# A fused attention and MLP block on one core: a half of chunk 1's second norm transposed by DMA, and two weight loads gated later

## The chip, the cores and the metric

The kernel runs on one NeuronCore of a Trainium2 chip. The metric is the device time of one execution in microseconds, the median of several runs. The profile shows one execution by itself.

## What is computed

One transformer block in bfloat16, for x of 1 x 2048 x 512. Attention is local and dilated: 32 heads of 16 features, and each position attends to itself and to the seven positions 2, 4, ..., 14 before it. The MLP is a gated one with F = 1376 hidden features.

```python
def _A_ref(x, wqkv, wo):            # S = 2048, D = 512, H = 32, Dh = 16
    W, dil = 8, 2
    q, k, v = ...(x @ wqkv) split in heads
    idx = pos[:, None] - (arange(W) * dil)[None, :]     # masked where < 0
    logits = einsum("bhsd,bhswd->bhsw", q, k[idx]) * Dh ** -0.5
    o = einsum("bhsw,bhswd->bhsd", softmax(logits), v[idx])
    return o.reshape(B, S, D) @ wo

def _B_ref(x, W_gate, W_up, W_down):
    gate = x @ W_gate
    return ((gate * (gate > 0)) * (x @ W_up)) @ W_down

h = x + _A_ref(_layernorm(x), wqkv, wo)
out = h + _B_ref(_layernorm(h), W_gate, W_up, W_down)
```

## The kernel before, in words

**Tiles and stages.** The 2048 rows are cut in four chunks of 512 rows, each of four blocks of 128 rows. All weights stay in on-chip memory once they are loaded. Each chunk goes through the same stages:

- *First norm* (the function `layernorm`, line 433). Mean and variance come from L467 on VectorE, the scale from two small ScalarE steps (L477, L480). The normalized row is written either by ScalarE (L499) or by VectorE (L502).
- *Transposing.* The matrix products want the features on the partitions, so each normalized block of 128 x 512 is transposed into a `quad` tile of 128 x 4 x 512. That happens in one of two ways. On TensorE it takes four transposes per block (L531, two blocks to a PSUM bank) and an eviction of the bank by ScalarE (L547). By DMA it takes one transposing transfer per block on SP's queue (L520). The table `DMAT` (L378) lists the pairs of blocks that go by DMA: ('h',1,0) stands for the second norm ("h") of chunk 1, blocks 0 and 1. All pairs that it doesn't list go by TensorE.
- *Query, key and value products* (L572, four matmuls of 512 columns each). ScalarE evicts them (L580): queries into a `quad` tile, keys into `kT`, values into `vT`. `kT` and `vT` are one tile each for all four chunks.
- *Scores.* VectorE multiplies queries with the keys of four window offsets at once (L620; four products to a chunk, each over two of the four feature groups of `kT` and written to a `big` tile; chunk 0 has smaller ones, L635). TensorE sums over the features (L626, 16 matmuls for half of the window), and ScalarE takes the exponential (L684).
- *Denominator and weights.* In chunks 1 to 3 VectorE adds the two halves (L716) and TensorE sums them with one matmul (L701). ScalarE forms the reciprocal (L707, L710). In these chunks VectorE scales the weights (L728), and eight broadcasting DMAs on SP (L744) spread them over the features into a `big` tile; in chunk 0 the sums are scaled at the end (L783).
- *Weighted sum.* VectorE multiplies with the values (L776, L791 in chunk 0). A tree of three additions follows: in chunks 0 to 2 the first one is an accumulating DMA on POOL's queue (L819), the others are VectorE's (L779, and L813 for the last one in chunks 1 to 3).
- *Output product and residual.* Four output products (L855) take four matmuls each. In chunk 0 a fifth matmul per block adds x by the identity (L858) and ScalarE evicts the bank with a row sum (L864); in the others VectorE adds x (L866).
- *Second norm*: the row sum gives the mean (L448, VectorE), ScalarE squares (L456), then scale, normalized rows (L502, VectorE) and transposes as above.
- *MLP.* Up and gate products (L928, 20 of four matmuls in a chunk), evicted by ScalarE (L932 and, with the ReLU, L935), multiplied by VectorE (L956). The last 96 features of F go through a tail of their own (L895 to L914, with one DMA transpose). The down product (L978, 11 matmuls to a block) is evicted by ScalarE and added to x by a DMA on POOL in chunks 0 and 1 (L987, L1012), and added by VectorE in chunks 2 and 3 (L991).

**Loads of weights.** W_up and W_down ("ud" in `LATE`) aren't loaded in the set-up. A small gate operation `lg` on POOL (L836) copies a few elements from the tile of chunk 0's last sum into both weight tiles. The loads overwrite these elements and so must wait for the gate. Two transfers for W_up and then the ones for W_down are issued on SP after it (`f_load`).

**What sets the order.** The body of the kernel only collects operations. `Plan.order` (L115) then simulates the engines (TensorE, VectorE, ScalarE, POOL, SP) with the durations and the DMA model that the file states, and emits the operations in the order of their simulated starts. The table `RANK` (L18) gives every operation a rank by the number in which it was collected; each engine takes its operations strictly by rank. So the order on one engine is that of `RANK`, and the simulation only decides how the engines' lists are interleaved when they are emitted. The framework then draws the semaphore waits from the order of emission: what is emitted later and touches the same tile waits for what was emitted earlier.

All chunks are interleaved: while chunk 0 is in its MLP, chunk 1 is in its attention, and so on. TensorE's list around the change, with the times of the profile before: query, key and value products of chunks 0 to 2 up to 49, among them the scores of chunk 0 and 1; the four output products of chunk 0 from 49.5 to 55, each between other products; the value products of chunk 2; chunk 0's up and gate products from 65; its down products among chunk 1's output products (85 to 91); chunk 1's second norm, its eight transposes at 96.2, and its up and gate products behind them.

Of the kernel before, what the change touches and what calls it, by code (L numbers as in the profile page):

```python
# [16 lines left out]

RANK = [  # L18
# [38 lines left out]
]  # L57


# [33 lines left out]
class Plan:  # L93
# [9 lines left out]
    def add(self, key, *a, **k):  # L103
        op = Op(*a, **k)
        op.key = key
        op.seq = len(self.ops)
        if RANK:
            op.prio = RANK[op.seq]
        self.ops.append(op)
        for b in set(op.take) | set(op.use):  # L110
            b.left += 1
        return op


    def order(self):  # L115
        waiting = list(self.ops)
        free = {}
# [7 lines left out]
        while left:  # L125
# [27 lines left out]
            for eng, cands in best.items():  # L153
                first = min(t for t, _ in cands)
                t, op = min(
                    ((t, op) for t, op in cands if t <= first + self.LOOK.get(eng, 0.02)),
                    key=lambda x: (x[1].prio, x[1].seq),
                )
                if pick is None or t < pick[0]:
                    pick = (t, op)  # L160
            t, op = pick
            op.start, op.done = t, t + op.dur + op.lat
            held = 0.0
            if op.dq:
                at, sw, busy = t + op.dur + op.dq[0], free.get("DQ", 0.0), op.dq[1]
                if op.eng == "POOL":
                    late = 1.0 if at < free.get("DT", -1.0) + 0.3 else 0.0
                    at = free["DQ"] = max(at, sw) + late + busy
                else:
                    turn = 0.6 < busy < 0.9  # L170
                    at = max(at, free.get("DQ" + op.eng, 0.0))
                    if at < sw + (0.3 if turn else 0.0):
                        share = 0.03 if turn else 0.18
                        late = max(sw - at, 0.0)
                        at += busy / share if late * share >= busy else late + busy - late * share
                        free["DQ"] = sw + (1.65 if turn else 0.5 * busy)
                        held = at + op.lat - 4.5
                    else:
                        at += busy
                    free["DQ" + op.eng] = at  # L180
                    if turn:
                        free["DT"] = at
                op.done = at + op.lat
            free[op.eng] = max(t + op.dur, held)
# [18 lines left out]
def kernel(  # L203
# [11 lines left out]
    nc = tc.nc  # L215
# [4 lines left out]
    NT = D // P  # L220
# [9 lines left out]
    LATE = "ud"  # L230
# [5 lines left out]
    NFT = NFF + (1 if FTAIL else 0)  # L236
# [32 lines left out]
    wgu_sb = sb.tile([P, NT, 2, F], BF16, name="wgu_sb")  # L269
    wd_sb = sb.tile([P, NFT, D], BF16, name="wd_sb")  # L270
# [93 lines left out]
    add = plan.add  # L364
# [10 lines left out]
    NHALF = 6  # L375
    XT = (3.5, 3.65, 5.6, 6.1, 8.5, 8.9, 9.4, 9.9, 15.9, 17.4)
    WT = (7.55, 7.55, 5.0, 14.2, 18.7, 25.5, 22.0, 29.0)
    DMAT = (('h',2,0),('h',2,2),('h',3,0),('h',3,2),('h',1,0),('x',3,0),('x',3,2))  # L378

    EARLY = (1, 2, 3)  # L380

# [31 lines left out]
    wload = {n: [load(t)] for n, t in zip(("q", "k", "ab", "v", "o", "u", "g", "d"), WT)}  # L413
# [141 lines left out]
    for tk in range(NCK):  # L555
# [10 lines left out]
        for n, (c, t) in enumerate(seq):  # L566
# [16 lines left out]
            if tk == 0 and n < NHALF:  # L583

                a = None
                for i, (lo, hi, d0, d1, evs) in enumerate(((0, 2 * P, 0, 2, xev[0:2]), (0, 2 * P, 2, NT, []), (2 * P, CS, 0, NT, xev[2:]))):
                    a = add(("qk%s%d" % ("abc"[i], n), tk), "PE", MM * (d1 - d0) * (hi - lo) / CS + 0.005,
                            lambda f=f_mm, lo=lo, hi=hi, d0=d0, d1=d1: f(lo, hi, d0, d1),
                            evs + [wload["ab"][0] if i == 0 else wl, a, fills[-1]], pr - 5,
                            take=[mm], use=[xnT], lat=PEL if i == 2 else 0.0)  # L590
            else:
                a = add(("qkv%d" % n, tk), "PE", 4 * MM, f_mm, xev + [wl], pr, take=[mm], use=[xnT], lat=PEL)
# [9 lines left out]
        apr = base + 20  # L602
# [130 lines left out]
        ab, abd = Buf(ab_s), []  # L733
# [99 lines left out]
            if tk not in EARLY:  # L833
                oev[t] = add(("om%d" % t, tk), "DVE", D2, f_om, [m, rcd], tpr, take=[OT], use=[mt, rc], lat=DL)
        if tk == 0 and LATE:
            def f_lg(mt=mt):  # L836
                nc.gpsimd.tensor_copy(out=wgu_sb[0:1, :, 1, 0:1], in_=mt.t[0:1, 0:1, 0:NT].rearrange("p a s -> p s a"))
                nc.gpsimd.tensor_copy(out=wd_sb[0:1, :, 0:1], in_=mt.t[0:1, 0:1, 0:NFT].rearrange("p a s -> p s a"))

            lg = add(("lg", tk), "POOL", 0.3, f_lg, [oev[NT - 1]], apr, use=[mt], lat=0.1)  # L840
            for n in LATE:
                for i in range(2):
                    wload[n].append(add(("ld" + n, i), "SP", 0.45 + 0.1 * (n == "d" and i), lambda n=n, i=i: f_load(n, i),
                                        [lg], 0, lat=0.5, dq=(1.0, 1.74)))
        for t in range(NT):
            kdone["v", tk, t] = vd[t]

# [217 lines left out]
```

## Time and profile before

| | |
|---|---|
| time, median of 3 runs | 197.32 us (197.26 to 197.83) |
| the profiled execution, its own time | 195.9 us |
| span of the profiled execution | 193.9 us |
| TensorE busy | 189.1 us (98%) |
| VectorE busy | 147.4 us (76%) |
| ScalarE busy | 119.0 us (61%) |
| POOL busy | 16.9 us (9%) |

The span reaches from the first to the last instruction of the profiled execution; its own time is longer by what lies around that. The median belongs to other executions. In the lines of the profile, PE is TensorE, DVE is VectorE, ACT is ScalarE and SP issues DMAs; L and a number is a line of the kernel. A line of a timeline has the start and the length in microseconds (a group of like instructions in one line), the engine, the line, the operation, the tiles out<-in, and in brackets a wait ahead of it and what released it. In a line of the chain of waits the two numbers are the start and the length of one step.

### The profile page before, as it was taken

To read this page: it belongs to the slowest core of one execution; us is meant where nothing else is said; L and a number is where in the kernel's file an instruction comes from. 1 tells how busy PE (TensorE), PEld (TensorE's weight loads), DVE (VectorE), ACT (ScalarE), POOL (GpSimd) and SP (SyncE) were. 2 spreads that over 40 slices of the span, in tenths; PEclk is the share of its full clock that TensorE was granted. 3 is DMA by queue.
4 is the path that set the end of the run, shared out by engine and by line. 5 is a ranking of instruction groups with operands and counts; after the bars stand their busy time and mean duration, and the time that the engine had idled before them with its cause. 6 is when DMAs were issued, how large, how long until landed. Compare 5 with 4: busy or idle time off the path is not lost.

```text
span 193.9 us, 3084 instructions
## 1 busy us (share of the span) xinstructions
PE 189.1 (98%) x1133; PEld 98.7 (51%) x1133; DVE 147.4 (76%) x237; ACT 119.0 (61%) x245; POOL 16.9 (9%) x35
## 2 busy tenths in 40 slices
PE   7999999999999999999999999999999999999994
PEld 7886454554345445444444454444444645544543
DVE  6999999979999999988998658899965321404432
ACT  3689999973997777665346858505658803445600
POOL 3000002510000023100033110003000000000000
PEclk9999999999999999999999999999999999999999
DMA  6889475999508657926366998222400460004103
GB/s 200 240 261 392 133 182 96 196 194 261 217 0 192 163 108 149 176 50 156 79 126 132 193 183 175 54 54 40 71 0 0 99 198 3 0 0 136 53 3 108
DMA packets 25214, 24.61 MB, mean 127 GB/s; under 512 B 11408, under 2 KB 21488, under 8 KB 25200
## 3 DMA queue, kind: packets, MB, share of 16 engines
q1 hardware_dynamic: 22176, 16.26, 30.5%
q0 software_dynamic: 2304, 7.34, 20.9%
q10 hardware_dynamic: 720, 0.82, 1.2%
q8 instruction: 9, 0.15, 0.3%
q14 instruction: 5, 0.04, 0.1%
HBM read 8.42 MB, written 2.10 MB: 54 GB/s over the span
## 4 chain that ended last, share of the span: by engine, by line
PE 88%; DVE 4%; ACT 3%; DMA 1%; issue 1%; DVEq 0%
PE bank L928 36%; PE bank L978 20%; PE bank L572 14%; PE bank L855 7%; PE bank L626 4%; PE bank L895 3%; PE bank L421 3%; DVE big L620 2%; PE bank L531 2%; ACT row L499 2%; DMA quad<-row 1%; DVE big L779 1%; ACT kT L580 1%; DVE quad L783 1%; PE bank L858 0%
## 5 line engine op out<-in xcount | busy, mean ns | idle before, releaser
L928 PE MATMUL bank<-quad,wgu_sb 128*128 128x512 bf16 x320 | 71.7, 379 | 0.0
L928 PEld LDWEIGHTS <-wgu_sb 128*128 128x128 bf16 x320 | 31.1, 98 | 37.1 <-issue 0.8
L978 PE MATMUL bank<-wd_sb,gT 128*128 128x512 bf16 (+3 forms) x198 | 39.7, 355 | 0.0
L935 ACT ACTIVATE gr<-bank 128x512 bf16<-128x512 f32 x40 | 23.7, 604 | 15.5 <-PE bank L928 13.0
L932 ACT CAST up_sb<-bank 128x512 bf16<-128x512 f32 x40 | 23.0, 590 | 15.8 <-PE bank L928 13.9
L572 PE MATMUL bank<-quad,wqk_sb 128*128 128x512 bf16 (+1 forms) x152 | 29.6, 345 | 0.8 <-DMA quad<-row 0.4
L978 PEld LDWEIGHTS <-gT 128*128 128x128 bf16 (+1 forms) x198 | 18.4, 98 | 19.8 <-issue 0.4
L620 DVE TENSOR_TENSOR big<-quad,kT 128x4096 bf16<-128x4096 bf16 x12 | 27.3, 2285 | 1.0 <-ACT kT L580 0.9
L776 DVE TENSOR_TENSOR big<-big,vT 128x4096 bf16<-128x4096 bf16 x12 | 27.2, 2283 | 0.0
L572 PEld LDWEIGHTS <-wqk_sb 128*128 128x128 bf16 x152 | 16.7, 113 | 11.3 <-issue 1.1
L956 DVE TENSOR_TENSOR gT<-gr,up_sb 128x1024 bf16<-128x1024 bf16 x20 | 13.7, 688 | 9.4 <-ACT gr L935 7.4
L991 DVE TENSOR_TENSOR row<-x_sm,bank 128x512 bf16<-128x512 bf16 (+2 forms) x10 | 5.5, 579 | 19.0 <-PE bank L978 19.0
L819 POOL DMA_DIRECT2D big<-big x12 | 10.5, 931 | 84.0 <-DVE big L776 55.9
L779 DVE TENSOR_TENSOR big<-big 128x1024 bf16<-128x1024 bf16 (+2 forms) x24 | 17.2, 730 | 0.6 <-DMA big<-big 0.3
L572 PE MATMUL bank<-quad,wv_sb 128*128 128x512 bf16 x64 | 15.7, 380 | 0.0
L855 PE MATMUL bank<-wo_sb,quad 128*128 128x512 bf16 x64 | 15.0, 379 | 0.1
L547 ACT COPY quad<-bank 128x1024 bf16<-128x1024 bf16 (+1 forms) x10 | 8.6, 888 | 5.6 <-PE bank L531 5.6
L456 ACT ACTIVATE row<-x_sm,mv 128x512 bf16<-128x512 bf16 x12 | 8.6, 716 | 4.3 <-DVE mv L448 4.2
L866 DVE SCALAR_TENSOR_TENSOR x_sm<-x_sm,bank 128x512 bf16<-128x512 bf16 x12 | 8.1, 684 | 3.9 <-PE bank L855 3.9
L467 DVE BATCH_NORM_STATS2 st<-x_sm 128x6 f32<-128x512 bf16 x16 | 10.4, 676 | 0.6 <-DMA x_sm<-in_A_x_dram 0.5
L580 ACT CAST kT<-bank 128x512 bf16<-128x512 f32 x16 | 9.2, 598 | 2.6 <-DVE big L620 1.9
L580 ACT CAST quad<-bank 128x512 bf16<-128x512 f32 x16 | 8.9, 599 | 2.5 <-PE bank L572 2.5
(77 smaller groups left out, 169.9 us busy)
## 6 DMA issues: line engine op xcount, KB each, us to landing
big<-big POOLq DMA_DIRECT2D x12, 512.0 KB, 4.9
big<-ex SPq DMA_DIRECT2D x32, 128.0 KB, 2.9
wgu_sb<-in_B_W_gate_dram SPq DMA_DIRECT2D x2, 688.0 KB, 9.3
wgu_sb<-in_B_W_up_dram SPq DMA_DIRECT2D x2, 688.0 KB, 8.3
wd_sb<-in_B_W_down_dram SPq DMA_DIRECT2D x2, 640.0 KB, 6.3
x_sm<-in_A_x_dram SPq DMA_DIRECT2D x2, 512.0 KB, 6.3
x_sm<-up_sb POOLq DMA_DIRECT2D x4, 256.0 KB, 4.4
out_dram<-x_sm SPq DMA_DIRECT2D x4, 256.0 KB, 2.3
```

Of the source, the lines that this page charges most:

```text
L572: nc.tensor.matmul(mm.t[:, lo:hi], lhsT=wv_sb[:, dt, t:D:NT] if c == 2 else wqk_sb[:, dt, c * D + t:(c + 1) * D:NT], rhs=xnT.t[:, dt, lo:h ...
L580: nc.scalar.copy(out=o, in_=mm.t[:])
L620: V.tensor_tensor(out=pb.t[:].rearrange("p (t w) s -> p t w s", t=2), in0=q4, in1=k4, op=ALU.mult)
L776: V.tensor_tensor(out=mt.t[:], in0=ab.t[:], in1=v8, op=ALU.mult)
L779: V.tensor_tensor(out=mt.t[:, 0:n, :], in0=mt.t[:, 0:n, :], in1=mt.t[:, n:2 * n, :], op=ALU.add)
L819: nc.gpsimd.dma_start(mt.t[:, 0:4, :], mt.t[:, 4:8, :], accum_op=ALU.add)
L855: nc.tensor.matmul(od.t[:], lhsT=OT.t[:, t, j * P:(j + 1) * P], rhs=wo_sb[:, t, :], start=(t == 0), stop=(t == NT - 1 and tk not in RPE))
L928: nc.tensor.matmul(mm.t[:fs, lo:hi], lhsT=wgu_sb[:, dt, g, ft * P: ft * P + fs], rhs=hnT.t[:, dt, lo:hi], start=(dt == 0), stop=(dt == NT ...
L932: nc.scalar.copy(out=ub.t[:fs, i, :], in_=um.t[:fs, :])
L935: nc.scalar.activation(out=gr.t[:fs, i, :], in_=gm.t[:fs, :], func=ACT.Relu)
L956: V.tensor_tensor(out=gt.t[:fs, 0:n, :], in0=gr.t[:fs, 0:n, :], in1=ub.t[:fs, 0:n, :], op=ALU.mult)
L978: nc.tensor.matmul(od.t[:, c0:c1], lhsT=gts[ft].t[:fs, ft % 2, j * P:(j + 1) * P], rhs=wd_sb[:fs, ft, c0:c1], start=(ft == 0), stop=(ft == ...
```

## The change

Four things are edited:

- `DMAT` gains ('h',1,2): blocks 2 and 3 of chunk 1's second norm are transposed by two DMAs on SP's queue and no longer by eight transposes on TensorE and an eviction on ScalarE.
- The gate of the weight loads depends on all four sums of chunk 0 and no longer on the last one alone. It copies from the tile of the sums (`OT`) into W_up's tile only; W_down's tile isn't written any more.
- The loads of W_down depend, in the plan, on chunk 1's eight broadcasts as well (`abd` with tk == 1), and so stand behind them on SP's queue.
- The planner's model of the DMAs has other constants, and `RANK` is another list throughout (748 entries in place of 749), so that the order on the engines differs from its second line of numbers on.

```diff
@@ RANK: another list @@
...
@@ Plan.order, DMA model @@
-                    late = 1.0 if at < free.get("DT", -1.0) + 0.3 else 0.0
+                    late = 3.0 if at < free.get("DT", -1.0) + 0.8 else 0.0
...
-                    if turn:
+                    if turn or 1.7 < busy < 1.8:
                         free["DT"] = at
...
-    DMAT = (('h',2,0),('h',2,2),('h',3,0),('h',3,2),('h',1,0),('x',3,0),('x',3,2))
+    DMAT = (('h',2,0),('h',2,2),('h',3,0),('h',3,2),('h',1,0),('x',3,0),('x',3,2),('h',1,2))
...
         if tk == 0 and LATE:
-            def f_lg(mt=mt):
-                nc.gpsimd.tensor_copy(out=wgu_sb[0:1, :, 1, 0:1], in_=mt.t[0:1, 0:1, 0:NT].rearrange("p a s -> p s a"))
-                nc.gpsimd.tensor_copy(out=wd_sb[0:1, :, 0:1], in_=mt.t[0:1, 0:1, 0:NFT].rearrange("p a s -> p s a"))
-
-            lg = add(("lg", tk), "POOL", 0.3, f_lg, [oev[NT - 1]], apr, use=[mt], lat=0.1)
+            def f_lg(OT=OT):
+                nc.gpsimd.tensor_copy(out=wgu_sb[0:1, :, 1, 0:1], in_=OT.t[0:1, :, 0:1])
+
+            lg = add(("lg", tk), "POOL", 0.2, f_lg, list(oev.values()), apr, use=[OT], lat=0.1)
             for n in LATE:
                 for i in range(2):
                     wload[n].append(add(("ld" + n, i), "SP", 0.45 + 0.1 * (n == "d" and i), lambda n=n, i=i: f_load(n, i),
-                                        [lg], 0, lat=0.5, dq=(1.0, 1.74)))
+                                        [lg], 0, lat=1.0, dq=(1.0, 1.74)))
+        if tk == 1 and "d" in LATE:
+            for op in wload["d"]:
+                op.deps += abd
```

74 rows, old and new, of the table RANK are left out of this document.

## The prediction

> **What bounds the kernel now.** I read the page's busy rows first.
>
> ```profile
> span 193.9 us, 3084 instructions
> ...
> PE 189.1 (98%) x1133; PEld 98.7 (51%) x1133; DVE 147.4 (76%) x237; ACT 119.0 (61%) x245; POOL 16.9 (9%) x35
> ```
>
> TensorE is busy for 98% of the span. So a microsecond counts if it is TensorE work or a TensorE wait. The chain that ended last, in order of time, shows where it waits:
>
> ```profile
> 49.51 1.04 PE bank L855 x4
> ...
> 65.17 6.15 PE bank L928 x28
> ...
> 96.17 0.45 PE bank L531 x8
> ...
> 181.56 9.59 PE bank L978 x66
> ```
>
> From 49.51 to 191.15 (181.56 + 9.59) the chain never leaves TensorE: whatever the change adds or takes there is gained or lost in full, and a wait of another engine counts only where it reaches TensorE. Before 49.51 I read TensorE's timeline (start, length, instructions):
>
> ```profile
> 33.54 1.03 PE L572 MATMUL bank<-quad,wqk_sb 128*128 128x512 bf16 x4 [0.42 <-DMA quad<-row]
> 34.41 1.03 PE L572 MATMUL bank<-quad,wv_sb 128*128 128x512 bf16 x4
> ...
> 39.40 8.80 PE L572 MATMUL bank<-quad,wqk_sb 128*128 128x512 bf16 x40
> 48.39 1.05 PE L626 MATMUL bank<-big,sel 128*32 128x512 bf16 x16 [0.20 <-ACT kT L580]
> 49.51 1.04 PE L855 MATMUL bank<-wo_sb,quad 128*128 128x512 bf16 x4
> ...
> 51.78 1.05 PE L626 MATMUL bank<-big,sel 128*32 128x512 bf16 x16
> 52.76 1.04 PE L855 MATMUL bank<-wo_sb,quad 128*128 128x512 bf16 x4
> ...
> 53.85 1.03 PE L572 MATMUL bank<-quad,wv_sb 128*128 128x512 bf16 x4
> 54.71 0.38 PE L701 MATMUL bank<-row,same 128*128 128x512 bf16 x1
> ```
>
> Starts give paces: four matmuls of 512 columns take 0.87 (33.54 to 34.41); their row's 1.03 runs 0.16 past that. The forty thus end at 39.40 + 8.80 - 0.16 = 48.04, 0.216 each. An output product with its residual takes 1.09 (52.76 to 53.85), the sixteen L626 matmuls 0.98 (51.78 to 52.76) and some 0.09 ahead of them. So TensorE loses 0.35 ahead of 48.39 and 0.14 ahead of 49.51; that is nearly all that could be won beside removed work.
>
> VectorE and ScalarE in that stretch:
>
> ```profile
> 41.62 2.29 DVE L620 TENSOR_TENSOR big<-quad,kT 128x4096 bf16<-128x4096 bf16 x1 [0.91 <-ACT kT L580]
> ...
> 45.44 2.29 DVE L620 TENSOR_TENSOR big<-quad,kT 128x4096 bf16<-128x4096 bf16 x1
> ...
> 49.03 0.43 DVE L783 TENSOR_TENSOR quad<-big,rec 128x512 bf16<-128x512 bf16 x1
> 49.37 4.49 DVE L620 TENSOR_TENSOR big<-quad,kT 128x4096 bf16<-128x4096 bf16 x2
> 53.78 0.14 DVE L448 TENSOR_SCALAR mv<-sm 128x1 f32<-128x1 f32 x1
> 53.84 0.41 DVE L716 TENSOR_TENSOR row<-ex,ex 128x512 bf16<-128x512 bf16 x1
> ...
> 59.68 1.38 DVE L502 TENSOR_SCALAR row<-x_sm,mv,rs 128x512 bf16<-128x512 bf16 x4
> ```
> ```profile
> 35.09 1.52 ACT L499 ACTIVATE row<-x_sm,nb,rs 128x512 bf16<-128x512 bf16 x2
> 36.51 1.06 ACT L580 CAST quad<-bank 128x512 bf16<-128x512 f32 x2
> 37.46 0.65 ACT L710 ACTIVATE rec<-lnd 128x512 bf16<-128x512 f32 x1
> 37.99 1.93 ACT L547 COPY quad<-bank 128x1024 bf16<-128x1024 bf16 x2
> ...
> 40.94 0.59 ACT L580 CAST kT<-bank 128x512 bf16<-128x512 f32 x1
> ...
> 47.76 0.58 ACT L580 CAST kT<-bank 128x512 bf16<-128x512 f32 x1 [1.91 <-DVE big L620]
> ...
> 51.10 0.68 ACT L864 ACTIVATE x_sm<-bank 128x512 bf16<-128x512 f32 x1
> 51.59 0.28 ACT L864 ACTIVATION_READ_ACCUMULATOR x_sm<-bank 128x1 f32 x1
> ```
>
> Two rows matter most. VectorE stood 0.91 for a key copy into kT, and ScalarE stood 1.91, until the third score product L620 of chunk 1 ended (45.44 + 2.29 = 47.73), to write keys into kT. That copy is of chunk 2, whose columns the product doesn't read; a product spans two feature groups of kT, so the wait seems drawn for the whole stretch between them. Which copies stand behind which products is set by the order of emission, and that is what the new RANK changes.
>
> **The change part by part** (lines as in the kernel before).
>
> *Transposes.* Eight L531 transposes leave TensorE: -0.45 by the row at 96.17. Their eviction leaves ScalarE, which is off the chain. In their place SP issues two more DMA transposes; the four of chunk 1 follow each other, as four did here:
>
> ```profile
> 26.94 5.25 SPq L520 DMA_TRANSPOSE quad<-row  x4
> ```
> ```profile
> DMA to landing us min/median/max: 2.4/2.5/2.7
> ```
>
> So 1.31 each, and the last lands 3 x 1.31 + 2.5 = 6.4 after the first issue. From the end of the chunk's last output product to there, by rows of this kernel:
>
> ```profile
> 90.17 5.99 PE L978 MATMUL bank<-wd_sb,gT 128*128 128x512 bf16 x27
> ```
> ```profile
> 93.37 0.73 DVE L502 TENSOR_SCALAR row<-x_sm,mv,rs 128x512 bf16<-128x512 bf16 x2
> ```
>
> Product's end (90.17) to first row operation (93.37) is 3.2, the row and its signal 0.45, then 6.4: 10.05. In the changed order TensorE meanwhile has 44 down matmuls and one L626 group, 44 x 0.216 + 1.07 = 10.57. Cover 0.5, cost nothing; without that cover the delay counts one for one. What stands before them on SP, the broadcasts L744 and a tail transpose, waits for VectorE steps of the time ahead of the output product and is gone by then.
>
> The Trainium skill, "VectorE: DVE Perf Modes", The three transpose paths, with its rules for kernel authors, speaks against this edit: a full 128 x 128 transpose belongs on TensorE where PSUM will do as its target. The page's prices are 390 ns there and 1309 ns by DMA. The trace has 56 ns in a stream of eight, and 1.31 us of issue for four blocks at once; by the row the edit saves 0.45 as long as the landing is covered, by the rule it would lose.
>
> *Held weights.* The gate copy on POOL now follows the last of chunk 0's four sums instead of one; by the emitted order W_down follows chunk 1's broadcasts on SP. Behind the gate copy on POOL stand only chunk 1's accumulating transfers L819, due some twenty microseconds later. Chunk 0's should land sooner with no weight load beside them:
>
> ```profile
>   DVE big L779: 0.3, 1
> ...
> DMA to landing us min/median/max: 4.5/4.9/9.3
> ```
>
> They land in 4.5 to 9.3, but VectorE waited 0.3 for them in all, so nothing is gained. The up weights go out behind the last sum, from about 49.3. They and the gate weights took up to 9.5:
>
> ```profile
> DMA to landing us min/median/max: 8.2/8.8/9.5
> ```
>
> With the second issue at 50.5 that is 60, five ahead of their first use (65.17): hidden. W_down, issued behind the eight broadcasts, is needed only after chunk 1's output product: hidden too.
>
> *The new order, 41 to 66.* The key copy for the second L620 is now, behind TensorE's second product from 33.54 (two end at 34.41 + 0.87 = 35.28; 0.12 to ScalarE): two copies, L499, a copy, L547, a copy, L710, L547, the key copy. By ScalarE's starts (copy 0.48, L499 0.71, L547 0.95, L710 0.53): 35.40 + 4 x 0.48 + 0.71 + 2 x 0.95 + 0.53 + 0.59 = 41.05, against 40.94 + 0.59 = 41.53. VectorE is 0.47 earlier, and chunk 0's last sum is there at 49.03 + 0.43 - 0.47 = 48.99; TensorE has its bank for L626 at 48.04 and starts chunk 0's output product at 49.10 instead of 49.51: -0.41.
>
> Then comes a wait that before doesn't have there. A key copy of chunk 2 is emitted behind chunk 1's *fourth* L620, and waits for it; behind that copy on ScalarE stands the residual sum L864; and on VectorE its L448 now stands *ahead* of the next L620. So: fourth L620 from 48.90 to 51.19; copy, 51.22 + 0.48; L864 with its accumulator 0.77, 52.47; L448. VectorE stands 51.10 to 52.5. The next L620 (2.2) ends 54.75, L716 ends 55.16 (0.41), L701 starts at 55.21. TensorE gets there at 49.10 + 2 x 1.09 + 1.07 + 1.09 + 0.87 = 54.31: +0.90. Bounds: 0, if the copy isn't held, to 1.4, the whole stand.
>
> VectorE then comes to the normalized rows of chunk 0 at 60.4 instead of 59.68 (two L620 of 2.2 and short ones of 0.9 behind 55.1); the second row is there at 61.2; TensorE, with L701, an output product, four products and an L626 group behind 55.21, at 61.0: +0.25 with the row after it.
>
> *Chunk 1's output product.* The eight down matmuls ahead of it now stand behind it:
>
> ```profile
> 84.99 1.89 PE L978 MATMUL bank<-wd_sb,gT 128*128 128x512 bf16 x8
> 86.72 3.62 PE L855 MATMUL bank<-wo_sb,quad 128*128 128x512 bf16 x16
> ```
> ```profile
> 85.50 0.42 DVE L813 TENSOR_TENSOR quad<-big 128x512 bf16<-128x512 bf16 x1
> ```
>
> TensorE asks for the sums at 86.72 - 1.73 + 0.75 = 85.74. VectorE, 0.72 late and with one gating product L956 (0.60) less ahead, has them at 85.50 + 0.42 + 0.05 + 0.12 = 86.09, or some 0.35 sooner if the small pauses of that stretch close up: 0 to 0.35, I take 0.15.
>
> *Sum:* -0.45 - 0.41 + 0.90 + 0.25 + 0.15 = **+0.44** against a span of 193.9. The profiled execution took 195.9; the median of the runs is 197.32. The 1.4 between them isn't in this span; I carry the difference over: 197.32 + 0.4 = **197.7 us**. After chunk 1 the order of waits is as before, and so is the end: two 128-column pieces behind a 512 one.
>
> **Rivals.**
>
> *Faster: the stand doesn't reach TensorE.* The first two terms alone: -0.86, 196.5. For it: TensorE never waited for VectorE after 49.51. Against: in the trace of before L716 ended at 53.84 + 0.41 = 54.25, only 0.46 ahead of L701, and the stand is 1.4; the waits are written in the program.
>
> *Slower: the DMA-transposed half lands late.* Place: TensorE's first up product of chunk 1. It decides once the last landing is more than 0.5 behind my 10.05. Fourteen landings between 2.4 and 2.7 speak against; for it speaks that L819 took 9.3 instead of 4.5 beside weight loads. If a landing doubles, 2.5 more less 0.5: 199.7; a typical slip of 1.5 gives 198.7. This is also how the skill's rule would turn out.
>
> *Slower: VectorE stays late.* If its pauses grow with the denser order, chunk 1's output product waits the full 0.35 and as much again: +1.0, 198.3.
>
> *It doesn't do what it says:* the gate only delays a load that is hidden anyway, and without the order's effects -0.45 is left: 196.9. I give it no weight of its own beside the first rival.
>
> **How the numbers follow.** Forecast 0.50, faster rival 0.15, late landing 0.20, VectorE late 0.12, unnamed 0.03. A difference under 0.3% (0.6 us) can't be told from none. The forecast's own range, 197.2 to 198.1, reaches over that bound with a tenth; so faster 0.15, same 0.47, slower 0.38. Low end 196.6, by the faster rival; high end 198.8, past the third and the typical second.
>
> **What would show it.** Right: a VectorE wait of 1.2 to 1.5 for L864 (L866 after) near 51, behind a ScalarE wait for L620; a TensorE wait for L716 of about 0.9 near 54; 64 transposes on TensorE; first up product some 0.7 later than 65.17. Wrong: no wait at L701 (faster rival); a TensorE wait for a DMA transpose near 100 (second); one for L813 over 0.5 near 86 (third).

## The result

The changed kernel takes 198.2 us (median of 14 runs, 196.93 to 200.12) against 196.91 us for the kernel before (14 runs, 196.21 to 197.83): a ratio of 1.0071, with a 95% interval of 1.0048 to 1.0094. It is slower by 1.3 us, where the forecast was 0.4 slower. One of the 14 runs, that of 200.12, counts as slow and is left out of the ratio. The profiled executions took 197.99 and 195.9, with these spans and busy rows after the change:

```profile
span 195.9 us, 3055 instructions
...
PE 189.1 (97%) x1125; PEld 97.8 (50%) x1125; DVE 147.2 (75%) x237; ACT 117.9 (60%) x244; POOL 18.6 (9%) x34
```

TensorE's busy time is 189.1 before and after and so tells nothing here; its waits do. TensorE's waits in the changed kernel (in total, times, longest):

```profile
PE bank L572 <- ACT quad L580: 1.1, 1, 1.1
...
PE bank L701 <- DVE row L716: 0.7, 1, 0.7
PE bank L857 <- DVE quad L813: 0.6, 1, 0.6
PE bank L531 <- DVE row L502: 0.3, 1, 0.3
```

Lines behind the edited gate have moved by two: L857 is the output product, L866 the residual sum on ScalarE, L930 the up and gate products, L980 the down product. To see what each wait costs, I lay TensorE's timelines beside each other at points that stand for the same work. After the change:

```profile
34.24 1.89 PE L572 MATMUL bank<-quad,wqk_sb 128*128 128x512 bf16 x8 [1.14 <-ACT quad L580]
...
49.80 1.04 PE L857 MATMUL bank<-wo_sb,quad 128*128 128x512 bf16 x4
...
55.84 0.38 PE L701 MATMUL bank<-row,same 128*128 128x512 bf16 x1 [0.69 <-DVE row L716]
...
66.42 3.63 PE L930 MATMUL bank<-quad,wgu_sb 128*128 128x512 bf16 x16
...
87.46 3.19 PE L857 MATMUL bank<-wo_sb,quad 128*128 128x512 bf16 x14 [0.55 <-DVE quad L813]
90.49 5.34 PE L980 MATMUL bank<-wd_sb,gT 128*128 128x512 bf16 x24
...
101.09 3.62 PE L930 MATMUL bank<-quad,wgu_sb 128*128 128x512 bf16 x16
```

Of before, two rows are needed beside those in the prediction:

```profile
65.10 6.22 PE L928 MATMUL bank<-quad,wgu_sb 128*128 128x512 bf16 x28
...
99.49 3.62 PE L928 MATMUL bank<-quad,wgu_sb 128*128 128x512 bf16 x16
```

The last store of each, before and then after:

```profile
191.50 0.35 ACTq L997 DMA_DIRECT2D out_dram<-row  x1
```
```profile
193.09 0.35 ACTq L999 DMA_DIRECT2D out_dram<-row  x1
```

| stretch, us | before | after | difference | forecast |
|---|---|---|---|---|
| start of the span to chunk 3's first product | 33.54 | 34.24 | +0.70 | 0 |
| to chunk 0's first output product | 15.97 | 15.56 | -0.41 | -0.41 |
| to L701 | 5.20 | 6.04 | +0.84 | +0.90 |
| to chunk 0's first up product | 10.39 | 10.58 | +0.19 | +0.25 |
| to the end of chunk 1's output product | 23.34 | 24.07 | +0.73 | +0.15 |
| to chunk 1's first up product | 11.05 | 10.60 | -0.45 | -0.45 |
| to the issue of the last store | 92.01 | 92.00 | 0 | 0 |
| to the end of the span | 2.4 | 2.8 | +0.4 | 0 |

(In before, eight down products of 0.216 stand ahead of chunk 1's output product, which the change puts behind it: 1.73 is moved from the fifth stretch, 25.07, to the sixth, 9.32, so that like stands beside like.) The differences add up to 2.0, the difference of the spans. Without the first row they give 1.3, that of the medians. The first row varies from profile to profile, as shown below. Of the rest two rows are off: chunk 1's output product and the end.

**The stand.** VectorE and then ScalarE in the changed kernel at the place where the prediction put it:

```profile
49.57 2.28 DVE L620 TENSOR_TENSOR big<-quad,kT 128x4096 bf16<-128x4096 bf16 x1
53.10 0.15 DVE L448 TENSOR_SCALAR mv<-sm 128x1 f32<-128x1 f32 x1 [1.24 <-ACT x_sm L866]
53.17 2.28 DVE L620 TENSOR_TENSOR big<-quad,kT 128x4096 bf16<-128x4096 bf16 x1
55.37 0.42 DVE L716 TENSOR_TENSOR row<-ex,ex 128x512 bf16<-128x512 bf16 x1
```
```profile
51.89 0.58 ACT L580 CAST kT<-bank 128x512 bf16<-128x512 f32 x1 [1.33 <-DVE big L620]
52.37 0.60 ACT L866 ACTIVATE x_sm<-bank 128x512 bf16<-128x512 f32 x1
```

The key copy waits 1.33 for chunk 1's fourth product, the residual sum stands behind the copy, and VectorE stands 1.24 for the sum. In before this place had no wait.

**The collision.** The eight broadcasts L744 of chunk 2 on SP, before and then after:

```profile
84.60 6.25 SPq L744 DMA_DIRECT2D big<-ex  x8
```
```profile
78.45 11.81 SPq L744 DMA_DIRECT2D big<-ex  x8
```

And how long chunk 1's last accumulating transfer L819 (issued on POOL at 78.54 before, 78.38 after) took to land, before and then after:

```profile
DMA to landing us min/median/max: 4.5/4.5/4.5
```
```profile
DMA to landing us min/median/max: 7.8/7.8/7.8
```

The new order scales chunk 2's first weights six microseconds earlier. So four broadcasts start just when the last two L819 run, and the last one takes 3.3 longer to land. Not all of that is the broadcasts' doing: in the new order the last L819 also follows the one ahead of it after 2.2 (3.4 in before), and where the broadcasts are moved away (runs 2, 6 and 7 below) it takes 6.0. VectorE waits for it:

```profile
86.25 0.69 DVE L779 TENSOR_TENSOR big<-big 128x1024 bf16<-128x1024 bf16 x1 [1.00 <-DMA big<-big]
86.97 0.43 DVE L813 TENSOR_TENSOR quad<-big 128x512 bf16<-128x512 bf16 x1
```

L813 ends at 87.40, and TensorE starts the rest of its output product at 87.46.

**The first row of the table.** The profile puts the wait of 1.14 at 34.24 down to a ScalarE copy, and names the last one ahead of it. But the one that TensorE's instruction depends on had ended at 32.63:

```profile
32.05 0.58 ACT L580 CAST quad<-bank 128x512 bf16<-128x512 f32 x1 [0.37 <-PE bank L572]
```

The instruction also depends on the four DMA transposes of chunk 3. They were issued from 26.94 in before (the prediction shows the line) and from 27.64 now, behind the broadcasts of chunk 0 (before, then after):

```profile
21.06 5.78 SPq L744 DMA_DIRECT2D big<-ex  x8
```
```profile
21.03 6.51 SPq L744 DMA_DIRECT2D big<-ex  x8
27.64 5.25 SPq L520 DMA_TRANSPOSE quad<-row  x4
```

SP's list is the same in both kernels up to there. Chunk 3's first product starts at 33.54, 34.08, 34.57 and 35.05 in the four profiles taken in the order of before, and at 33.69 to 35.14 in the nine in the new order. The two ranges overlap, so the 0.70 isn't shown to be of the change.

The spans can be freed of this row: from chunk 3's first product to the end it is 160.4 in before and 161.65 after. Counted in this way, each later kernel differs from before by an amount that lies within the interval of its own runs: +1.3 in run 8, +1.4 in run 5, +1.2 in run 2, +6.0 in run 3, +0.6 in runs 7 and 11, +0.4 in run 10, 0 in runs 1 and 4, -0.5 in run 6 and -0.9 in run 9.

### The profile page after: what moved, and what is told of

It is laid out like the page before. It is cut to its first block, busy times and chain, and to the rows that moved or that the text cites. A ratio compares the mean times of both kernels' runs of the same rounds, so it can differ in the third digit from the quotient of the medians.

```text
span 195.9 us, 3055 instructions
## 1 busy us (share of the span) xinstructions
PE 189.1 (97%) x1125; PEld 97.8 (50%) x1125; DVE 147.2 (75%) x237; ACT 117.9 (60%) x244; POOL 18.6 (9%) x34
## 4 chain that ended last, share of the span: by engine, by line
PE 70%; DVE 11%; DMA 7%; ACT 4%; issue 3%; SPq 2%; DVEq 0%
PE bank L930 26%; PE bank L980 20%; PE bank L572 13%; PE bank L857 6%; DVE big L620 5%; DMA big<-big 4%; DVE big L776 3%; PE bank L897 2%; DMA x_sm<-in_A_x_dram 2%; PE bank L626 1%; DVE big L779 1%; SPq L744 1%; DMA big<-ex 1%; ACT kT L580 1%; ACT quad L547 1%
## 5 line engine op out<-in xcount | busy, mean ns | idle before, releaser
L930 PE MATMUL bank<-quad,wgu_sb 128*128 128x512 bf16 x320 | 72.2, 379 | 0.0
L930 PEld LDWEIGHTS <-wgu_sb 128*128 128x128 bf16 x320 | 31.0, 98 | 36.8 <-issue 0.8
L980 PE MATMUL bank<-wd_sb,gT 128*128 128x512 bf16 (+3 forms) x198 | 39.4, 355 | 0.0
L937 ACT ACTIVATE gr<-bank 128x512 bf16<-128x512 f32 x40 | 23.1, 601 | 14.1 <-PE bank L930 11.7
L934 ACT CAST up_sb<-bank 128x512 bf16<-128x512 f32 x40 | 22.8, 594 | 12.8 <-PE bank L930 8.8
L980 PEld LDWEIGHTS <-gT 128*128 128x128 bf16 (+1 forms) x198 | 18.4, 98 | 20.1 <-issue 0.4
L958 DVE TENSOR_TENSOR gT<-gr,up_sb 128x1024 bf16<-128x1024 bf16 x20 | 13.8, 691 | 16.9 <-ACT gr L937 9.9
L779 DVE TENSOR_TENSOR big<-big 128x1024 bf16<-128x1024 bf16 (+2 forms) x24 | 17.1, 732 | 1.3 <-DMA big<-big 1.2
L819 POOL DMA_DIRECT2D big<-big x12 | 10.5, 903 | 72.7 <-DVE big L776 48.2
L857 PE MATMUL bank<-wo_sb,quad 128*128 128x512 bf16 x64 | 15.5, 379 | 0.6 <-DVE quad L813 0.6
L989 ACT CAST up_sb<-bank 128x512 bf16<-128x512 f32 x8 | 4.5, 587 | 11.4 <-PE bank L980 10.6
```

What stands on the lines that cost most here:

```text
L779: V.tensor_tensor(out=mt.t[:, 0:n, :], in0=mt.t[:, 0:n, :], in1=mt.t[:, n:2 * n, :], op=ALU.add)
L857: nc.tensor.matmul(od.t[:], lhsT=OT.t[:, t, j * P:(j + 1) * P], rhs=wo_sb[:, t, :], start=(t == 0), stop=(t == NT - 1 and tk not in RPE))
L930: nc.tensor.matmul(mm.t[:fs, lo:hi], lhsT=wgu_sb[:, dt, g, ft * P: ft * P + fs], rhs=hnT.t[:, dt, lo:hi], start=(dt == 0), stop=(dt == NT ...
L934: nc.scalar.copy(out=ub.t[:fs, i, :], in_=um.t[:fs, :])
L937: nc.scalar.activation(out=gr.t[:fs, i, :], in_=gm.t[:fs, :], func=ACT.Relu)
L958: V.tensor_tensor(out=gt.t[:fs, 0:n, :], in0=gr.t[:fs, 0:n, :], in1=ub.t[:fs, 0:n, :], op=ALU.mult)
```

## The experiments

The stretches are those of the table. Edits of the order are edits of `RANK`, told as the list of the engine. The kernel before ran beside each.

**1. The key copy first.** On ScalarE, in the changed kernel:

```diff
 L580: chunk 2, query 0
-      chunk 2, query 3
+      chunk 2, key 2
       chunk 3, query 3
       chunk 1, value 3
-      chunk 2, key 2
+      chunk 2, query 3
```

> The changed kernel, with one key copy of chunk 2 (feature group 2) and one query copy exchanged on ScalarE, so that the key copy is emitted ahead of chunk 1's fourth L620 and no longer waits for it. Theory (the stand of VectorE behind L866 reaches TensorE and costs 0.84): VectorE's wait of 1.24 for L866 and TensorE's 0.69 at L701 are gone, the ratio to before falls from 1.007 to 1.003 (about 197.4 us with before at 196.9), or to 1.002 where the 0.19 of the late transposes goes too. Rival (the stand is hidden, and the loss lies in the late transposes of chunk 3 at 34 and the late sums of chunk 1 at 87): VectorE's wait goes and the time stays at 198.2, ratio 1.007.

Measured: 197.07 us, ratio 1.0013 (0.9986 to 1.0039). VectorE goes from product to product:

```profile
49.05 2.29 DVE L620 TENSOR_TENSOR big<-quad,kT 128x4096 bf16<-128x4096 bf16 x1
51.26 0.15 DVE L448 TENSOR_SCALAR mv<-sm 128x1 f32<-128x1 f32 x1
51.33 2.28 DVE L620 TENSOR_TENSOR big<-quad,kT 128x4096 bf16<-128x4096 bf16 x1
```

The stretch to L701 is 5.20 and that to the up product 10.40, both as in before. The fifth is 23.82 instead of 24.07, since VectorE isn't late as well. These three add up to 1.3, the ratio fell by 0.0058 (1.1 us). The time went the theory's way and not the rival's: one exchange of two copies takes back what the stand was said to cost.

**2. The broadcasts later.** On VectorE, in the changed kernel:

```diff
-L728 chunk 2, first half
 L958, L779, L779, L813, L813, L620, L958, L779, L958, L813, L779, L813
+L728 chunk 2, first half
 L728 chunk 2, second half
```

This is later than the expectation says: both halves of L728 now stand behind the last L813, while the kernel before has the first half ahead of three of these additions.

> The changed kernel, with chunk 2's first scaling L728 on VectorE put back behind chunk 1's last tree addition but one, where the kernel before has it, so that chunk 2's first broadcasts are issued behind chunk 1's accumulating transfers and not beside them. Theory (the transfers collide): the last L819 lands in 4.5 to 5 instead of 7.8, TensorE's wait for L813 near 87 (0.55) is gone and VectorE's 1.0 ahead of L779 too, the time falls by 0.55 to 0.7 to about 197.6, ratio 1.004. Rival (VectorE is late because of its stand at 51, whatever the transfers do): L813 stays late, TensorE's wait stays at 0.4 to 0.6, 198.2.

Measured: 197.93 us, 1.0049 (1.0023 to 1.0076). The wait for L813 is gone (fifth stretch 23.35 instead of 24.07). The last L819, though, took 6.0 to land and not 4.5 to 5:

```profile
DMA to landing us min/median/max: 6.0/6.0/6.0
```

That is early enough. But the sixth stretch is 11.23 instead of 10.60, with a wait that wasn't there:

```profile
PE bank L930 <- DMA quad<-row: 0.5, 1, 0.5
```
```profile
86.38 6.18 SPq L744 DMA_DIRECT2D big<-ex  x8
92.68 1.24 SPq L916 DMA_TRANSPOSE gT<-row  x1
94.03 5.62 SPq L520 DMA_TRANSPOSE quad<-row  x4
```

All eight broadcasts now end at 92.56 and the tail's transpose at 93.92, while VectorE writes the four rows from 92.98 on: SP has become what the four transposes wait for. By the profile 0.72 was won and 0.63 lost; the interval of the time alone reaches from the theory's 1.004 to the 1.007 of the change.

**3. The half by DMA alone.** The kernel before with

```diff
-    DMAT = (('h',2,0),('h',2,2),('h',3,0),('h',3,2),('h',1,0),('x',3,0),('x',3,2))
+    DMAT = (('h',2,0),('h',2,2),('h',3,0),('h',3,2),('h',1,0),('x',3,0),('x',3,2),('h',1,2))
```

> The kernel before with the transposing edit alone: blocks 2 and 3 of chunk 1's second norm go by two DMAs on SP's queue, everything else in the order of before. Theory (the edit is worth 0.45 only under a cover that the new order supplies): the first of four issues comes at 93.8 as before, the last lands 3 x 1.31 + 2.5 later, at 100.2, and TensorE asks for it at 99.49 - 0.45 = 99.0, so it waits 1.2 and the time rises by 0.7 to 0.8: 197.7, ratio 1.004. Rival (the landing is hidden in any order): minus 0.45, 196.5, ratio 0.998.

Measured: 202.6 us, 1.0291 (1.0259 to 1.0323). The side is right, the size is off by seven times. TensorE's wait, the landings of all L520, POOL's transfer at that time, and a table by stretches (TensorE, its weight loads, VectorE, ScalarE and POOL busy, the granted clock, the DMA share, GB/s):

```profile
103.96 5.30 PE L928 MATMUL bank<-quad,wgu_sb 128*128 128x512 bf16 x15 [4.23 <-DMA quad<-row]
```
```profile
DMA to landing us min/median/max: 2.4/2.4/5.1
```
```profile
98.38 0.86 POOL L819 DMA_DIRECT2D big<-big  x1 [18.44 <-DVE big L776]
```
```profile
98.00:99.60 1.60, 1.60 (x8) 0.58 (x6) 1.60 (x2) 0.00 (x0) 0.86 (x1) 1.00 0.41 82
99.60:103.90 4.30, 0.13 (x1) 0.00 (x0) 4.30 (x4) 1.57 (x3) 0.86 (x1) 1.00 1.04 187
103.90:105.90 2.00, 1.94 (x6) 0.80 (x7) 1.12 (x1) 0.00 (x0) 0.58 (x2) 0.59 0.99 188
105.90:107.90 2.00, 2.00 (x7) 0.74 (x6) 0.00 (x0) 0.00 (x0) 2.00 (x3) 0.56 0.69 131
```

The last of the four transposes was issued at 98.7, while POOL issued chunk 2's first L819, and landed in 5.1 instead of 2.4. In the changed kernel it was issued at 98.2, and that L819 only at 100.52, when it had all but landed. TensorE stood 4.2, and behind the stand its granted clock averaged 0.59 and 0.56 in two stretches of two microseconds: the seventh stretch is 1.68 longer (up product to last store 93.69 instead of 92.01). So the edit needs the cover that the new order gives it, and here a missed cover cost far more than the 1.2 by which the expectation had it missed. That the L819 delayed the landing is read from the two lying side by side in one profile; no run separates them.

**4. The held weights alone.** The kernel before with the gate of the change and W_down's loads behind chunk 1's broadcasts on SP (the last two parts of the change's diff). W_up thereby goes out first: in the kernel before, the second part of W_down is issued ahead of W_up (at 40.22 and 40.67, W_up from 42.09) and only its first part behind the broadcasts (62.15).

> The kernel before with the gate and the held weights alone: the gate follows all four sums of chunk 0, W_up goes out first, W_down behind chunk 1's broadcasts; the rest in the order of before. Theory (the loads are hidden either way): no difference over 0.2, ratio 0.999 to 1.001; up weights land some five microseconds ahead of their use, and the median landing of chunk 0's L819 stays at 4.5 to 5 with the 9.3 gone. Rival (the loads beside the sums cost time in before): VectorE's key products start earlier and the time falls by 0.3 to 0.5, ratio 0.998.

Measured: 196.79 us, 0.9986 (0.9963 to 1.0010): no difference. The stretches are those of before within 0.06. W_up landed 4.1 to 5.3 after its issue (8.2 to 8.5 in before), chunk 0's L819 in at most 8.1 instead of 9.3. Both are faster, and in neither profile does an engine wait for them.

**5. The half on TensorE again.** The changed kernel without ('h',1,2) in `DMAT`; the eight transposes stand ahead of the last eleven down products of chunk 0.

> The changed kernel in its new order, with the transposing edit alone undone: blocks 2 and 3 of chunk 1's second norm go by eight TensorE transposes and an eviction, ahead of the last eleven down products of chunk 0. Theory (the edit is worth 0.45 in the new order, and the profile's terms are all there is): 0.45 slower than the changed kernel, about 198.6, ratio to before 1.009. Rival (the landing has so little cover that in some executions it is late, which one profile doesn't show): the same as the changed kernel or faster, 197.4 to 198.2, ratio 1.003 to 1.007, and its runs lie closer together than the changed kernel's 196.9 to 200.1.

Measured: 198.22 us, 1.0073 (1.0049 to 1.0096), as fast as the changed kernel. Neither story holds: the sixth stretch is 11.04 instead of 10.60, so the transposes do cost 0.44, and the runs lie no closer together (196.89 to 201.29). The 0.44 comes back at a place that both stories had left out. The span ends at 196.2, 2.4 behind the issue of its last store as in before, and not 2.8:

```profile
193.79 0.35 ACTq L999 DMA_DIRECT2D out_dram<-row  x1
```

**6. Both mended.** The changed kernel with the exchange of run 1 and, on VectorE, L728 of chunk 2's first half behind the second of the three L958, ahead of the third L779: later than in the change, earlier than in run 2.

> The changed kernel with the key copy first on ScalarE (as in the run before) and chunk 2's first scaling L728 some four microseconds later on VectorE, behind the second gating product, so that its four broadcasts start when chunk 1's last L819 has landed, but end before SP is wanted for the transposes. Theory (stand and collision are what the change lost): no wait at L701, none for L813 near 86, none for the transposes: minus 0.41 and minus 0.45 are left, 196.0 to 196.4, ratio 0.996 to 0.998. Rival (the landings of the transposes are late in some executions, whatever the sums do): 197.0, ratio 1.000 to 1.002, with a spread of 2 or more.

Measured: 196.83 us, 1.0003 (0.9972 to 1.0034). The stretches are 15.56, 5.19, 10.40, 23.35 and 10.60: the waits of the stand, of the collision and of run 2 are all gone, -0.85 by the profile. Yet the time is that of before and misses the expectation by 0.4. The end is 2.8 again.

**7. The broadcasts between, alone.** The changed kernel with the second edit of run 6 only.

> The changed kernel with only the second of those two edits: chunk 2's first scaling L728 behind the second gating product. Theory (collision of broadcasts and L819): TensorE's wait for L813 (0.55) and VectorE's for the last L819 (1.0) are gone, and unlike the later place tried before, SP is free when the rows of chunk 1 are there, so no wait for a transpose comes instead: 0.7 less than the changed kernel, 197.5, ratio 1.003 to 1.004. Rival (SP or the landing takes it back as in that run): 198.0, ratio 1.005 or more.

Measured: 197.93 us, 1.0057 (1.0027 to 1.0087). The fifth stretch is 23.35 and the sixth 10.67, so by the profile the 0.7 is won and not given back. The time is less clear: against the changed kernel on the same chip (run 8) it is 0.9 less, against the first measurement 0.3, the ratio is nearer the rival's, and the intervals leave either. That the collision costs 0.7 therefore rests on the profiles (runs 2, 6 and 7), not on a difference of times.

**8. The changed kernel again.**

> The changed kernel once more, for a second profile and its times on the same chip as the others of this set. Theory (the start of chunk 3's products at 34.24 instead of 33.54 and the longer end of the span were chance, the rest is of the change): ratio 1.005 to 1.009; in the profile the waits at L701 (0.7) and for L813 (0.55) again, and first product of chunk 3 to first output product of chunk 0 again 15.56. Rival (the late transposes of chunk 3 belong to the change): first L626 of chunk 0 to the first product of chunk 3 again 15.2 to 15.3 against 14.6 in before.

Measured: 198.84 us, 1.0092 (1.0065 to 1.0120). The stretches 6.13, 10.57, 23.89 and 10.60 come back, and the second is 15.71. The end is 2.8 again, so it was no chance, and the theory fails there. Chunk 3's first product started at 35.14, later still, and 15.40 behind chunk 0's first L626, even more than the rival's 15.2 to 15.3. But this doesn't decide for the rival, since runs 3 and 4, in the order of before, have 15.22 and 15.18, and the starts there reach 35.05.

**The end.** All kernels with an end of 2.8 have one thing in common. In the program as it is built, the DMAs of SP and ScalarE take eight semaphores in turn, and SP waits for these one after another before the program ends (shortened):

```
SP  wait  DMAHW0, DMASW5
SP  wait  DMAHW1, DMASW4
...
SP  wait  DMAHW7, Activation
```

In before the last store has number 6; two more DMAs make it number 0, with seven waits behind it. The traces show them: what SP still passes once the last store has landed, before and then after (193.0 is 1.5 behind the issue of that store in before, 194.6 as much in the changed kernel):

```profile
L1060 SPq EVENT_SEMAPHORE  x2: 28/28/28, 193.0 to 193.1; - x2
```
```profile
L1062 SPq EVENT_SEMAPHORE  x8: 28/28/28, 194.6 to 195.0; - x8
```

Eight waits instead of two, some 0.06 apart, make the 0.4. Runs 9 to 11 set out to test this by changing the number of DMAs, run 10 without anything else.

**9. Both mended, one up load.** Run 6 with (in short)

```diff
-                wgu_sb[:, 2 * i:2 * i + 2, 1, :] <- w[:, 2 * i:2 * i + 2, :]   for i in 0, 1
+                wgu_sb[:, :, 1, :] <- w
```

> The kernel with both mends (key copy first, broadcasts between), and W_up loaded by one transfer instead of two. At its end a kernel waits on SP for its eight DMA semaphores one after the other, and the DMAs take these in turn; with one transfer less, the last output store is the last of the eight waited for and no longer the first. Theory (the closing waits behind the last landing cost some 0.06 each, and the two added transposes turned the order): from the issue of the last store to the end of the span 2.4 as in before and not 2.8; against the kernel with both mends 0.4 less: 196.3, ratio to before 0.998. Rival (the end's length is of another cause): 2.8 again, 196.8, ratio 1.000.

Measured: 196.0 us, ratio 0.9961 (0.9939 to 0.9984): faster than before and than the change. The span is 193.8 and the last store (three lines further down in this kernel):

```profile
191.39 0.35 ACTq L1002 DMA_DIRECT2D out_dram<-row  x1
```

2.4 behind it the span ends. The stretches are those of run 6.

**10. The kernel before with two more loads** (W_up in four transfers):

> The kernel before, with W_up loaded by four transfers instead of two, so that the last output store takes the first of the eight DMA semaphores, as in the changed kernel; the order of all engines is that of before. Theory (closing waits): 2.8 from the issue of the last store to the end of the span instead of 2.4, the rest as in before: 0.4 slower, 197.1, ratio 1.002. Rival (the longer end belongs to the changed order or to the DMA transposes themselves): 2.4, ratio 1.000.

Measured: 197.22 us, 1.0027 (1.0006 to 1.0049). The span ends at 195.4:

```profile
192.57 0.35 ACTq L998 DMA_DIRECT2D out_dram<-row  x1
```

2.8, in the order of before and without a DMA transpose more.

**11. The changed kernel with one up load:**

> The changed kernel with W_up loaded by one transfer instead of two and nothing else. Theory (closing waits): 2.4 at the end instead of 2.8, the stand and the collision as in the changed kernel: 0.4 less than it, 197.8 to 198.0, ratio 1.005 to 1.007, with the same waits at L701 (0.7) and for L813 (0.4 to 0.55). Rival: 2.8 at the end, ratio 1.007 to 1.009.

Measured: 197.52 us, 1.0031 (1.0012 to 1.0051), with 2.4 at the end, 6.05 to L701 and 23.86 to the end of chunk 1's output product. The gain on the changed kernel is 0.8, more than the end's 0.4; 0.2 of the rest is the fifth stretch, and what remains is within the intervals.

Over the thirteen profiles the end is 2.4 to 2.5 where the last store has semaphore 6 or 7 (before, runs 4, 5, 9, 11), and 2.7 to 2.8 where it has 0 (after, runs 1, 2, 3, 6, 7, 8, 10). The last store landed 1.5 after its issue in before, in the changed kernel and in runs 1, 3, 4, 5, 6 and 8, so the 0.4 lies behind the landing.

**A lower clock in some executions.** The mean granted clock of an execution was 0.983 to 0.991 in 11 of the 99 executions in the new order (runs 3, 4 and 10 have the order of before), three of them among the 14 of the changed kernel: 199.28, 199.84 and 200.12. In the 106 executions in the order of before for which it is on record, run 3 apart, it was never under 0.997. Run 3's profile, with a mean of 0.990, is the only one that shows such a case: a long stand of TensorE with a lower clock behind it. So it is likely, but not shown, that in the new order TensorE now and then stands for several microseconds. It isn't the added half alone, since run 5, which lacks it, has one such execution (201.29). No profile caught one in the new order, and where TensorE stands there is open.

## Why the prediction was right, and where not

- *The range and the direction* held: 198.2 lies in 196.6 to 198.8, and the slower side was forecast. The forecast's own range, 197.2 to 198.1, misses it by 0.1, and by 0.5 as a difference: the kernel before came out at 196.91 and not 197.32, so 1.3 stands against at most 0.8. The loss is three times the 0.44 of the sum. That the range still holds is partly luck: its upper end came from a late landing that neither profile of the changed kernel shows.
- *Transposes, -0.45:* right (-0.45; undone in run 5, 0.44 comes back). The cover was narrow, as worked out: in the changed kernel the fourth L520 landed some 10.1 behind the output product, where 10.05 was forecast, and no wait followed; in run 2 it was missed by 0.5. In the new order the edit was worth 0.45 less the 0.4 of the end, that is nothing (run 5), and without the new order it lost 5.7 (run 3). The Trainium skill, "VectorE: DVE Perf Modes", The three transpose paths, with its rules for kernel authors, has a full transpose on TensorE where PSUM will do as its target. In the order of before that was the better advice, though not by the Trainium skill's prices.
- *Held weights, nothing:* right (run 4).
- *The new order up to chunk 0's output product, -0.41:* right; it came in every profile of the new order (-0.26 to -0.41). That the product itself started 0.29 later and not 0.41 earlier is the first row of the table.
- *The stand, +0.90 with +0.25 behind it:* right, +0.84 and +0.19, and taken back by run 1. This was the step that reading the waits in the program, and not the trace alone, gave.
- *Chunk 1's output product, +0.15:* the step that failed. "VectorE, 0.72 late and with one gating product L956 (0.60) less ahead" reckons only with VectorE. What ended last was the DMA: the new order lets chunk 2's broadcasts start six microseconds earlier, beside chunk 1's last sums (landing 7.8, against 6.0 without the broadcasts and 4.5 in before). Run 7, with VectorE as late as in the change, takes the whole 0.7 away, so that lateness costs nothing by itself; run 1, without it, leaves 0.5 of the 0.7. The prediction had quoted the sums' landings of 4.5 to 9.3 and used them only where VectorE waited before. The rival "VectorE stays late" had the place and nearly the time (198.3), and its sign, a wait for L813 over 0.5, came (0.55), but the mechanism was another.
- *"and so is the end":* failed too, by 0.4. The program's last waits had not been read; two more DMAs shift which semaphore the last store has, and eight waits instead of two follow its landing. Runs 9 to 11 show it, run 10 without any other part of the change.
- *The late landing* as a rival: it didn't occur in the changed kernel's two profiles, but in run 3, at a price beyond what was given to it (1.0 to 2.0, with 5.7 measured), in part because the clock falls as well (1.7).

## What to carry to other kernels

When an order is changed, list the DMAs that move with it and ask for each what else will be on the queues at its new time; a wait that was short in the old trace is no evidence. Read the program's waits, not only the trace, for a copy that is emitted behind a reader of the same tile: exchanging two copies was worth 1.1 us here. A difference of a few tenths can come from the count of DMAs alone, so look at the time between the last store and the end of the span before crediting it to anything else.

## What the hardware showed beside this

- TensorE paid twice for a long wait. After 4.2 us without matmuls (run 3) its granted clock averaged 0.59 and 0.56 of full speed in the next two stretches of two microseconds, with 0.50 between 105.5 and 107.3, and 1.68 us were lost there. The wait of 1.14 in the changed kernel left the clock at 1.00. The Trainium skill, "TensorE: Matmul & The Clock Gate", Part 1, says that the array falls to half its clock after an idle window of about 3.4 us and needs a busy one to return. This trace agrees (4.2 us idle, then 0.50).
- A DMA transpose that landed in 2.4 took 5.1 beside an accumulating transfer (run 3), and an accumulating transfer that takes 6.0 in the same order without them (runs 2, 6 and 7) took 7.8 beside four broadcasts. In before it took 4.5, with more time behind the accumulating transfer ahead of it (3.4 instead of 2.2).
- The waits that close this program run one after another, some 0.06 apart: seven of them behind that of the last store cost 0.4 us more than one or none.
